# One written order for the loads, attention units and weight decodings of the opening, with the scaling of maxima and the reciprocals joined

## The chip, the cores and the metric

The kernel runs on one core of a Trainium2 chip. The metric is device time in microseconds (us) of one execution; of several runs the median is taken. The engines are named as the profile names them: PE (TensorE, matrix products; PEld its weight loads), DVE (VectorE), ACT (ScalarE), POOL (GpSimd) and SP (SyncE, whose queue issues every transfer of this kernel).

## What is computed

Three layers in a row, all in float32: windowed attention with 32 global tokens, a feed-forward layer with ELU, then a gated layer with an RMS norm.

```python
def reference(**kwargs):
    attn_out = _attn_ref(...)            # 4 batches, 8 heads, 512 local + 32 global tokens, head size 64
    x = attn_out.transpose(0, 2, 1, 3).reshape(B * S, H * D)      # 2176 tokens x 512
    x = _moe_ref(x, w_in, w_out)
    return _moe2_ref(x, w_gate, w_val, w_out, rms_g)

def _attn_ref(...):
    ...
    s_ll = np.where(np.abs(pos[:, None] - pos[None, :]) <= 32, s_ll, -1e9)
    s_l = np.concatenate([s_lg, s_ll], axis=-1)
    out_l = np.matmul(sm(s_l), np.concatenate([v_g, v_l], axis=2))
    # sm: e = exp(s - max); e / (sum(e) + 1e-9)

def _moe_ref(x, w_in, w_out):            # 512 -> 2048 -> 512
    h = x @ w_in
    return np.where(h > 0, h, np.exp(np.minimum(h, 0)) - 1) @ w_out

def _moe2_ref(x, w_gate, w_val, w_out, rms_g):
    xn = x / np.sqrt(mean(x * x) + 1e-6) * rms_g
    return (silu(xn @ w_gate) * (xn @ w_val)) @ w_out
```

The weights of the last two layers come as float64, 1 MB for 128 rows of two 512-column pieces.

## The kernel before

**Tiles and stages.** Local tokens are worked on in four blocks of 512 (one batch each). A block has four attention units of 128 tokens, so unit u belongs to block u // 4. The attention of the first block's units 0 to 3 runs ahead of everything else; units 4 to 7 run inside the feed-forward of block 0, and so on. After the fourth block comes the gated layer. The first 145 us or so hold the opening (units 0 to 3) and block 0, and the change lies in the first half of these.

**An attention unit** (lines 218 to 280): `a_S` makes two halves of scores (by `par`) in PSUM on PE; `a_E` takes the row maxima of each half on DVE (line 243), multiplies them by -1/8 (line 244), and lets ACT make the exponentials E (line 246); `a_T` turns E on PE (line 252) and ACT copies the result to ET (line 254); `a_PV` multiplies with the values (line 265); `a_N` adds 1e-9 to the sums (line 278), takes reciprocals (line 279) and scales the output into x (line 280), on DVE, one half after the other. `a_X` turns a whole block's x into xT on PE, with its high part on ACT (line 289) and its low part on DVE (line 290).

**A decoding** makes one 128x1024 piece of weights ready: ACT takes the absolute value of the float64's high word (line 83, "abs"), four DVE operations make the float32 of it (lines 90 to 93), ACT rounds to a high part (line 96, "hi") and DVE takes the low part (line 99, "lo"). Decodings are numbered in the order of `order1`: of each four, the first two are of `w_in` and serve four steps of a block, the other two are of `w_out` and serve two steps each. Two `dx` tiles hold the decodings under way, so the abs of decoding i + 2 waits for the lo of decoding i.

**A step j of a block** (16 in all, `moe_block`): `mm1` (line 132, 12 matmuls) makes h; `act1` makes g of it, with ReLU and exponential on ACT (lines 121, 122), a DVE operation (line 123), the high part on ACT (line 139) and the low part on DVE (line 140); `mm2` of the step before (line 146, 12 matmuls) adds to y. `att_slot` puts a unit among four steps: `a_S` and `a_E` in the first, behind `mm1`; `a_T` in the second, between the halves of `mm2`; `a_PV` and `a_N` in the third, behind `mm1`. The scores of unit 5 lie in step 4, those of unit 6 in step 8, those of unit 7 in step 12. Two PSUM buffers (tag `att`) serve `a_S`, `a_T` and `a_PV` of these units in turn, so the scores of unit 5 need the outputs of unit 4 read by `a_N`.

**What sets the order.** PE's order is written by the program. On DVE, ACT and SP a scheduler sets it, except in the opening, where DVE and ACT follow the program's lines (a `manual_schedule` from the casts of the constants to the lo of decoding 2). Each engine takes its instructions strictly in its own order: one that waits holds up all behind it. Step 0 to step 15 of block 0, with decodings 3 to 15, are the scheduler's. Line 75 issues a load of weights, line 205 one of a unit's keys and queries (`kq`), line 215 one of its values (`v`).

Of the kernel before, what the change touches and what calls it, by code (L numbers as in the profile page):

```python
# [42 lines left out]
def fused_kernel(ctx: ExitStack, tc: tile.TileContext, kq, vl, gkq, gv, w_in, w_out, w_gate, w_val, w_o2, rms_g, consts, out):  # L43
# [43 lines left out]

    def dec_bits(x, raw):
        word = words(raw)
        nc.vector.tensor_scalar(out=x, in0=x, scalar1=HI_MIN, scalar2=HI_MAX, op0=ALU.max, op1=ALU.min)  # L90
        nc.vector.tensor_scalar(out=i32(x), in0=i32(x), scalar1=3, scalar2=0x3FFFFFFF, op0=ALU.logical_shift_left, op1=ALU.bitwise_and)
        nc.vector.scalar_tensor_tensor(out=i32(x), in0=word[:, :, 1], scalar=-0x40000000, in1=i32(x), op0=ALU.bitwise_and, op1=ALU.bitwise_or)  # L92
        nc.vector.scalar_tensor_tensor(out=i32(x), in0=word[:, :, 0], scalar=29, in1=i32(x), op0=ALU.logical_shift_right, op1=ALU.bitwise_or)  # L93
# [989 lines left out]
```

## Time and profile before

| | us |
|---|---|
| median of 3 runs (899.44 to 900.13) | 899.59 |
| the profiled execution | 899.1 |
| its span in the profile | 897.3 |
| PE busy | 864.9 (96%) |
| DVE busy | 588.0 (66%) |
| ACT busy | 475.8 (53%) |

A span is the time from the first to the last instruction in the profile. Busy PE is not PE at its peak, since ends of matmuls are modelled; what counts here is where PE stands still, and in whose queue the instruction stands that it waits for. Of the 32 us in which PE is not busy, 22 lie in the first 70 us.

### The profile page before, as it was taken

What the parts mean: (1) busy time and instruction counts of PE and PEld (TensorE: products, weight loads), DVE (VectorE), ACT (ScalarE), POOL (GpSimd) and SP (SyncE); (2) the same over time, 40 slices, a digit from 0 to 9 for tenths busy, and PEclk for the clock granted to TensorE, in tenths of its full rate; (3) what the DMA queues carried; (4) which work ended last, traced back from release to release, by engine and by line L of the source; (5) the groups of instructions that cost most, each with busy time, mean ns of one, the idle gap of its engine ahead of it and who ended that gap; (6) DMA issues with size and microseconds to landing.
All of it is one profiled execution on the core that took longest, in us unless ns stands there. A gap on an engine that the chain in (4) does not pass through costs nothing.

```text
span 897.3 us, 16243 instructions
## 1 busy us (share of the span) xinstructions
PE 864.9 (96%) x6652; PEld 736.4 (82%) x6652; DVE 588.0 (66%) x983; ACT 475.8 (53%) x863; POOL 19.4 (2%) x22
## 2 busy tenths in 40 slices
PE   4789999999999999999999999999999999999997
PEld 3567877888888888677888899997999998899995
DVE  4899988777677764443488656885355776365642
ACT  4677664555564444333456655664455665355531
POOL 0000000000000000000110101000100000000000
PEclk8999999999999999999999999999999999999999
DMA  9786365966678742441405532233222232133200
GB/s 361 289 305 198 124 255 178 300 229 203 228 273 267 248 163 112 148 177 60 167 1 188 179 114 91 96 120 118 81 96 94 95 119 80 59 118 118 95 24 35
DMA packets 60225, 139.26 MB, mean 155 GB/s; under 512 B 4856, under 2 KB 30584, under 8 KB 57592
## 3 DMA queue, kind: packets, MB, share of 16 engines
q1 hardware_dynamic: 60152, 138.23, 44.7%
q8 instruction: 52, 0.85, 0.4%
q14 instruction: 21, 0.17, 0.1%
HBM read 115.15 MB, written 23.07 MB: 154 GB/s over the span
## 4 chain that ended last, share of the span: by engine, by line
PE 79%; DVE 11%; DMA 4%; ACT 3%; issue 1%; SPq 0%; POOL 0%; ACTq 0%
PE y L146 16%; PE A L739 15%; PE h L132 15%; PE o L745 15%; PE Q L739 11%; DMA kq<-in_kq 2%; DVE dx L93 2%; DVE dx L92 1%; PE s L234 1%; PE ptp L252 1%; DVE wA L99 1%; PE o L265 1%; PE hg L675 1%; DMA raw<-in_moe_w_out 1%; DVE dx L90 1%
## 5 line engine op out<-in xcount | busy, mean ns | idle before, releaser
L146 PE MATMUL y<-g,wA 128*128 128x512 f32 x768 | 197.3, 400 | 4.7 <-DVE g L140 4.1
L132 PE MATMUL h<-xT,wA 128*128 128x512 f32 x768 | 186.5, 391 | 1.7 <-DVE xT L290 1.7
L146 PEld LDWEIGHTS y<-g,wA 128*128 128x128 f32 x768 | 140.0, 189 | 40.2 <-DVE g L140 6.0
L132 PEld LDWEIGHTS h<-xT,wA 128*128 128x128 f32 x768 | 143.5, 188 | 32.7 <-DVE xT L290 2.4
L739 PE MATMUL A<-xc,wS 128*128 128x384 f32 (+1 forms) x864 | 155.9, 328 | 1.7 <-ACT t L931 0.9
L739 PEld LDWEIGHTS A<-xc,wS 128*128 128x128 f32 x864 | 145.0, 188 | 6.6 <-ACT t L931 1.3
L745 PE MATMUL o<-wB,p 128*128 128x512 f32 x612 | 147.3, 392 | 0.7 <-DVE p L750 0.3
L745 PEld LDWEIGHTS o<-wB,p 128*128 128x128 f32 x612 | 113.6, 188 | 24.7 <-DVE p L750 2.5
L739 PE MATMUL Q<-xc,wS 128*128 128x384 f32 (+1 forms) x648 | 115.3, 326 | 0.0
L739 PEld LDWEIGHTS Q<-xc,wS 128*128 128x128 f32 x648 | 107.8, 188 | 0.0
L595 DVE TENSOR_TENSOR wS<-wraw,wS 128x1024 fp32r<-128x1024 f32 x63 | 78.5, 1246 | 36.2 <-ACT wS L594 36.0
L754 DVE TENSOR_TENSOR t<-t,Q 128x384 f32<-128x384 f32 (+1 forms) x108 | 55.9, 528 | 37.2 <-PE Q L739 24.0
L594 ACT CAST wS<-wraw 128x1024 fp32r<-128x1024 f32 x63 | 65.9, 1050 | 19.6 <-PE Q L739 11.4
L121 ACT ACTIVATE e<-h 128x512 f32<-128x512 f32 x48 | 29.0, 605 | 69.8 <-PE h L132 69.7
L139 ACT CAST g<-e 128x512 fp32r<-128x512 f32 x64 | 39.8, 621 | 47.3 <-DVE e L123 30.8
L123 DVE SCALAR_TENSOR_TENSOR e<-e,h 128x512 f32<-128x512 f32 x48 | 32.5, 678 | 33.3 <-ACT e L122 33.3
L140 DVE TENSOR_TENSOR g<-e,g 128x512 fp32r<-128x512 f32 x64 | 43.8, 684 | 9.4 <-ACT g L139 9.1
L750 DVE TENSOR_TENSOR p<-p,p 128x384 fp32r<-128x384 f32 x36 | 20.0, 557 | 43.1 <-ACT p L749 43.1
L83 ACT ACTIVATE dx<-raw 128x1024 f32<-128x1024 f32 x34 | 39.2, 1157 | 15.9 <-DMA raw<-in_moe_w_gate 6.0
L90 DVE TENSOR_SCALAR dx<-dx 128x1024 f32<-128x1024 f32 x34 | 23.2, 688 | 33.7 <-ACT dx L83 33.7
L246 ACT ACTIVATE E<-s,mx 128x128 f32<-128x128 f32 x128 | 34.8, 385 | 17.2 <-DVE mx L244 17.2
L92 DVE SCALAR_TENSOR_TENSOR dx<-raw,dx 128x1024 int32<-128x1024 int32 x34 | 41.9, 1239 | 0.6
(173 smaller groups left out, 867.1 us busy)
## 6 DMA issues: line engine op xcount, KB each, us to landing
wraw<-wS SPq DMA_DIRECT2D x63, 512.0 KB, 3.2
raw<-in_moe_w_out SPq DMA_DIRECT2D x14, 1024.0 KB, 7.6
raw<-in_moe_w_in SPq DMA_DIRECT2D x8, 1024.0 KB, 6.0
raw<-in_moe_w_gate SPq DMA_DIRECT2D x6, 1024.0 KB, 6.6
raw<-in_moe_w_val SPq DMA_DIRECT2D x6, 1024.0 KB, 5.7
wS<-raw SPq DMA_DIRECT2D x48, 128.0 KB, 2.4
gvr<-in_gv SPq DMA_DIRECT2D x8, 640.0 KB, 4.7
wS<-dx SPq DMA_DIRECT2D x36, 128.0 KB, 2.1
```

The costliest lines, as they stand in the source:

```text
L83: ins = nc.scalar.activation(x, f(words(raw)[:, :, 1]), AF.Abs)
L92: nc.vector.scalar_tensor_tensor(out=i32(x), in0=word[:, :, 1], scalar=-0x40000000, in1=i32(x), op0=ALU.bitwise_and, op1=ALU.bitwise_or)
L132: nc.tensor.matmul(h[:, :n], W1[c, G][:, ws, o:o + P], xT[c][:, xs, :n], start=(k == 0), stop=(k == 11))
L139: nc.scalar.copy(g[:, 0, :n], e[:, :n])
L140: nc.vector.tensor_tensor(out=g[:, 1, :n], in0=e[:, :n], in1=f(g[:, 0, :n]), op=ALU.subtract)
L146: nc.tensor.matmul(ys[dc][:, :n], W2[j][:, ws, dc * P:(dc + 1) * P], g[:, gs, :n], start=(j == 0 and k == 0), stop=(j == 15 and k == 2))
L246: nc.scalar.activation(e[par][:, pr, :], ss[par][:, pr, :], AF.Exp, bias=mx[:, par, pr:pr + 1], scale=SCALE)
L594: nc.scalar.copy(t[:, :, 0, :], raw)
L595: nc.vector.tensor_tensor(out=t[:, :, 1, :], in0=raw, in1=f(t[:, :, 0, :]), op=ALU.subtract)
L739: nc.tensor.matmul(ps[:, :n], w[:, 2 * (q % 4) + c, ws, :], x[:, c, xs, :n], start=(first and c == 0 and z == 0), stop=(c == 1 and z == 2) ...
L745: nc.tensor.matmul(o, p[:, pp, t * P:(t + 1) * P], Wo[j][:, ww, :], start=(first and z == 0), stop=(last and z == 2))
L754: nc.vector.tensor_tensor(out=t, in0=t, in1=ps, op=ALU.add)
```

## The change

The opening and steps 0 to 3 of block 0 are written out in two lists: `LOADS` for SP's queue, and `STEPS` for PE, DVE and ACT together. The helpers are cut into single operations for it (`dec_bit` is one of the four DVE operations of a decoding; `e_max`, `e_scale`, `e_exp`; `n_add`, `n_rec`, `n_mul`; `x_tr`, `x_hi`, `x_lo`), and `moe_block(0, ...)` begins at step 4. In `STEPS` a name is an operation and a number: mx, sc, exp, T, ET, PV, ad, rc, N belong to a unit (a and b are its halves), abs, ba, bb, bc, bd, hi, lo to a decoding, relu, ex, stt, ghi, glo to a step. Seven decodings (0 to 6) stand in the list, 5 ahead of 4. What follows the list on DVE and ACT is still the scheduler's, which may also put later operations between those of the list.

In every unit, of the list or not, the two multiplications by -1/8 are one (both halves, 128x8), and so are the two reciprocals; both maxima then come ahead of any exponential, and both sums ahead of any scaling of outputs. The condition that decodings in block 0 are issued after the last part of xT (`issue_after`) is gone.

```diff
+        def e_max(u, par):
+            if u not in mx_t:
+                mx_t[u] = small.tile([P, 2, 4], F32, tag="st", name="mx")
+            nc.vector.tensor_reduce(out=mx_t[u][:, par, :], in_=s_t[u][par], axis=AX.X, op=ALU.max)
+
+        def e_scale(u):
+            nc.vector.tensor_scalar(out=mx_t[u], in0=mx_t[u], scalar1=-SCALE, scalar2=None, op0=ALU.mult)
...
         def a_E(u):
-            ss = s_t.pop(u)
-            mx = small.tile([P, 2, 4], F32, tag="st", name="mx")
-            e = [ap_.tile([P, 4, P], F32, tag=f"E{par}", name="E") for par in range(2)]
-            for par in range(2):
-                nc.vector.tensor_reduce(out=mx[:, par, :], in_=ss[par], axis=AX.X, op=ALU.max)
-                nc.vector.tensor_scalar(out=mx[:, par, :], in0=mx[:, par, :], scalar1=-SCALE, scalar2=None, op0=ALU.mult)
-                for pr in range(4):
-                    nc.scalar.activation(e[par][:, pr, :], ss[par][:, pr, :], AF.Exp, bias=mx[:, par, pr:pr + 1], scale=SCALE)
-            e_t[u] = e
+            e_max(u, 0)
+            e_max(u, 1)
+            e_scale(u)
+            e_exp(u, 0)
+            e_exp(u, 1)
...
+        def a_N(u):
+            n_add(u, 0)
+            n_add(u, 1)
+            n_rec(u)
+            n_mul(u, 0)
+            n_mul(u, 1)
...
-        def moe_block(b, slot, after=None):
+        def moe_block(b, slot, j0=0, ys=None, prev=None):
...
+        LOADS = """
+            mk kq0 ident kq1 raw0 kq2 v0 raw1 kq3 v2 v1 raw2 v3 raw3 v4 raw5 kq4 raw6 raw4
+        """.split()
+        STEPS = """
...
+            bd6 ghi3 glo3 hi6 rc4 N4b lo6 N4a
+        """.split()
...
+        with tc.manual_schedule(engines={mybir.EngineType.SP}):
+            for what in LOADS:
+                start_load(what)
         with tc.manual_schedule(engines={mybir.EngineType.DVE, mybir.EngineType.Activation}):
...
+            for what in STEPS:
+                start_step(what)
+                if what in ("lo2", "lo3", "lo5", "lo6"):
+                    w1_load()
...
             if part == 2:
-                with tc.issue_after(last[0].ins), tc.issue_after(last[1].ins):
-                    w1_decode()
+                w1_decode()
...
-        moe_block(0, slot0)
+        moe_block(0, slot0, 4, y0, gs_[3])
```

**The order at three places.** From the scores of unit 5 on, PE has the same instructions in the same order as before. First, the head of SP's queue: before, the loads of values alternate with those of keys and queries.

```order
L205 DMA kq0_102<-in_kq 128x1408
L349 DMA ident_83<-in_consts 128x128
L350 DMA mk_104<-in_consts 128x384
L75 DMA raw_108<-in_moe_w_in 128x2x512
L215 DMA v0_110<-in_vl 128x2080
L205 DMA kq0_116<-in_kq 128x1408
L215 DMA v0_118<-in_vl 128x2080
L75 DMA raw_120<-in_moe_w_in 128x2x512
```

And the head of SP's queue now:

```order
L453 DMA mk_103<-in_consts 128x384
L213 DMA kq0_111<-in_kq 128x1408
L455 DMA ident_83<-in_consts 128x128
L213 DMA kq0_114<-in_kq 128x1408
L75 DMA raw_116<-in_moe_w_in 128x2x512
L213 DMA kq0_118<-in_kq 128x1408
L223 DMA v0_120<-in_vl 128x2080
L75 DMA raw_122<-in_moe_w_in 128x2x512
```

The masks and the keys and queries of units 0 to 2 moved ahead of the first values.

Second, DVE around the end of unit 4, whose two scalings (`x` from `o` and `st`) set free the PSUM that the scores of unit 5 are written to. Before, they stand among decodings 4 (`dx_794`, `wA_800`) and 5 (`dx_881`, `wA_887`):

```order
L99 TENSOR_TENSOR wA_800<-dx_794,wA_800 128x2x512
L278 TENSOR_SCALAR st_860<-o_826 128x4
L93 SCALAR_TENSOR_TENSOR dx_881<-raw_645,dx_881 128x1024
L279 RECIPROCAL st_860<-st_860 128x4
L123 SCALAR_TENSOR_TENSOR e_818<-e_818,h_805 128x512
L279 RECIPROCAL st_860<-st_860 128x4
L90 TENSOR_SCALAR dx_924<-dx_924 128x1024
L280 TENSOR_TENSOR x_859<-o_825,st_860 128x4x64
L280 TENSOR_TENSOR x_859<-o_826,st_860 128x4x64
L99 TENSOR_TENSOR wA_887<-dx_881,wA_887 128x2x512
```

Now (`dx_903`, `wA_917` are decoding 6, `dx_1018` is decoding 7; `g_914` belongs to step 3, `e_941` to step 4):

```order
L97 SCALAR_TENSOR_TENSOR dx_903<-raw_142,dx_903 128x1024
L95 SCALAR_TENSOR_TENSOR dx_1018<-raw_664,dx_1018 128x1024
L525 TENSOR_TENSOR g_914<-e_906,g_914 128x512
L299 RECIPROCAL st_863<-st_863 128x8
L131 SCALAR_TENSOR_TENSOR e_941<-e_941,h_928 128x512
L97 SCALAR_TENSOR_TENSOR dx_1018<-raw_664,dx_1018 128x1024
L306 TENSOR_TENSOR x_920<-o_829,st_863 128x4x64
L107 TENSOR_TENSOR wA_917<-dx_903,wA_917 128x2x512
L306 TENSOR_TENSOR x_920<-o_812,st_863 128x4x64
```

The scalings of unit 4 moved behind all of decoding 6, the four bit operations of decoding 7, and the DVE operation of step 4.

Third, DVE around the maxima of unit 6, for which its exponentials, and then its transposes on PE in step 9, wait. Before:

```order
L99 TENSOR_TENSOR wA_1218<-dx_1212,wA_1218 128x2x512
L99 TENSOR_TENSOR wA_1320<-dx_1314,wA_1320 128x2x512
L123 SCALAR_TENSOR_TENSOR e_1236<-e_1236,h_1223 128x512
L243 TENSOR_REDUCE mx_1285<-s_1243 128x4
L243 TENSOR_REDUCE mx_1285<-s_1244 128x4
L90 TENSOR_SCALAR dx_1371<-dx_1371 128x1024
L90 TENSOR_SCALAR dx_1455<-dx_1455 128x1024
L244 TENSOR_SCALAR mx_1285<-mx_1285 128x4
```

Now:

```order
L131 SCALAR_TENSOR_TENSOR e_1227<-e_1227,h_1214 128x512
L97 SCALAR_TENSOR_TENSOR dx_1444<-raw_1169,dx_1444 128x1024
L251 TENSOR_REDUCE mx_1276<-s_1234 128x4
L251 TENSOR_REDUCE mx_1276<-s_1235 128x4
L91 TENSOR_SCALAR dx_1485<-dx_1485 128x1024
L148 TENSOR_TENSOR g_1231<-e_1227,g_1231 128x512
L107 TENSOR_TENSOR wA_1450<-dx_1444,wA_1450 128x2x512
L254 TENSOR_SCALAR mx_1276<-mx_1276 128x8
```

The scaling of unit 6's maxima stood behind decodings 0 to 11 and the first operation of 12 and 13; now it stands behind decodings 0 to 13 and the first operation of 14.

## Rows read from the trace of the kernel before

**Rows 1.** Order of time on PE: start us, busy us, [idle before and its releaser].

```profile
36.32 1.64 PE L288 MATMUL xtp<-ident,x 128*128 128x128 f32 x13 [0.73 <-DVE x L280]
...
50.33 1.80 PE L146 MATMUL y<-g,wA 128*128 128x512 f32 x5 [2.56 <-DVE g L140]
...
66.37 2.81 PE L146 MATMUL y<-g,wA 128*128 128x512 f32 x11 [0.96 <-DVE g L140]
...
71.83 0.40 PE L228 MATMUL s<-masks,identr 128*32 128x256 bf16 x8
...
106.63 1.04 PE L252 MATMUL ptp<-ident,E 128*128 128x128 f32 x8
```

**Rows 2.** Stretches: start:end us, length, busy of PE, PEld, DVE, ACT, POOL, PEclk, DMA share, GB/s.

```profile
48.00:50.00 2.00, 0.00 (x0) 0.00 (x0) 2.00 (x3) 1.84 (x4) 0.00 (x0) 1.00 0.97 373
...
52.00:54.00 2.00, 2.00 (x10) 1.68 (x10) 1.97 (x4) 1.91 (x6) 0.00 (x0) 0.50 1.02 418
```

**Rows 3.** DVE by line, 0 to 63.9 us: xcount | busy us, mean ns | idle before, releaser.

```profile
L92 DVE SCALAR_TENSOR_TENSOR dx<-raw,dx 128x1024 int32<-128x1024 int32 x6 | 7.4, 1242 | 0.1
L93 DVE SCALAR_TENSOR_TENSOR dx<-raw,dx 128x1024 int32<-128x1024 int32 x6 | 7.3, 1218 | 0.1
...
L99 DVE TENSOR_TENSOR wA<-dx,wA 128x1024 fp32r<-128x1024 f32 x5 | 6.1, 1212 | 2.3 <-ACT wA L96 2.3
L90 DVE TENSOR_SCALAR dx<-dx 128x1024 f32<-128x1024 f32 x7 | 4.7, 681 | 9.8 <-ACT dx L83 9.8
...
L91 DVE TENSOR_SCALAR dx<-dx 128x1024 int32<-128x1024 int32 x6 | 4.1, 690 | 0.1
L290 DVE TENSOR_TENSOR xT<-xtp,xT 128x512 fp32r<-128x512 f32 x4 | 2.5, 684 | 1.0 <-ACT xT L289 1.0
L123 DVE SCALAR_TENSOR_TENSOR e<-e,h 128x512 f32<-128x512 f32 x3 | 2.0, 660 | 0.0
L279 DVE RECIPROCAL st<-st 128x4 f32<-128x4 f32 x10 | 1.7, 175 | 0.3
L244 DVE TENSOR_SCALAR mx<-mx 128x4 f32<-128x4 f32 x10 | 1.7, 166 | 0.3
...
L140 DVE TENSOR_TENSOR g<-e,g 128x512 fp32r<-128x512 f32 x2 | 1.4, 682 | 0.0
```

**Rows 4.** DVE by line, 0 to 104.25 us, the same columns.

```profile
L92 DVE SCALAR_TENSOR_TENSOR dx<-raw,dx 128x1024 int32<-128x1024 int32 x12 | 14.6, 1227 | 0.1
L93 DVE SCALAR_TENSOR_TENSOR dx<-raw,dx 128x1024 int32<-128x1024 int32 x12 | 14.5, 1215 | 0.1
L99 DVE TENSOR_TENSOR wA<-dx,wA 128x1024 fp32r<-128x1024 f32 x12 | 14.5, 1212 | 2.4 <-ACT wA L96 2.3
L90 DVE TENSOR_SCALAR dx<-dx 128x1024 f32<-128x1024 f32 x14 | 9.4, 681 | 9.8 <-ACT dx L83 9.8
...
L91 DVE TENSOR_SCALAR dx<-dx 128x1024 int32<-128x1024 int32 x12 | 8.1, 684 | 0.1
...
L140 DVE TENSOR_TENSOR g<-e,g 128x512 fp32r<-128x512 f32 x8 | 5.4, 679 | 0.0
```

**Rows 5.** Order of time on DVE.

```profile
46.13 1.21 DVE L93 SCALAR_TENSOR_TENSOR dx<-raw,dx 128x1024 int32<-128x1024 int32 x1
47.27 1.27 DVE L243 TENSOR_REDUCE mx<-s 128x4 f32<-128x512 f32 x2
48.47 1.20 DVE L99 TENSOR_TENSOR wA<-dx,wA 128x1024 fp32r<-128x1024 f32 x1
...
63.24 0.74 DVE L280 TENSOR_TENSOR x<-o,st 128x256 f32<-128x256 f32 x2
...
104.19 0.16 DVE L244 TENSOR_SCALAR mx<-mx 128x4 f32<-128x4 f32 x1
```

**Rows 6.** Order of time on ACT.

```profile
104.44 2.18 ACT L246 ACTIVATE E<-s,mx 128x128 f32<-128x128 f32 x8 [0.39 <-DVE mx L244]
```

**Rows 7.** Stretches, as in rows 2.

```profile
20.00:22.00 2.00, 1.06 (x64) 0.84 (x64) 1.86 (x7) 2.00 (x7) 0.00 (x0) 0.88 1.00 419
```

More of the change, by code (lines that the diff above doesn't have):

```diff
@@ L86, in dec_abs, with dec_bit @@
         return x
[L88 to L93 removed]
+    def dec_bit(k, x, raw):
+        word = words(raw)
+        if k == "a":
+            nc.vector.tensor_scalar(out=x, in0=x, scalar1=HI_MIN, scalar2=HI_MAX, op0=ALU.max, op1=ALU.min)
+        elif k == "b":
+            nc.vector.tensor_scalar(out=i32(x), in0=i32(x), scalar1=3, scalar2=0x3FFFFFFF, op0=ALU.logical_shift_left, op1=ALU.bitwise_and)
+        elif k == "c":
+            nc.vector.scalar_tensor_tensor(out=i32(x), in0=word[:, :, 1], scalar=-0x40000000, in1=i32(x), op0=ALU.bitwise_and, op1=ALU.bitwise_or)
+        else:
+            nc.vector.scalar_tensor_tensor(out=i32(x), in0=word[:, :, 0], scalar=29, in1=i32(x), op0=ALU.logical_shift_right, op1=ALU.bitwise_or)
+    def dec_bits(x, raw):
+        for k in "abcd":
+            dec_bit(k, x, raw)
     def split_hi(dst, t):
@@ L269, in a_N, with pv @@
-        def a_N(u):
-            b, T = u // 4, u % 4
-            if T == 0:
+        def pv(u, par, pool, tag):
+            ets, v = et_t.pop((u, par)), v_t[u]
+            o = pool.tile([P, 4, 65], F32, tag=tag, name="o")
+            for pr in range(4):
+                for i in range(4):
+                    nc.tensor.matmul(o[32 * i:32 * i + 32, pr, :], ets[:, pr * P + 32 * i:pr * P + 32 * i + 32], v[:, i, 2 * pr + par, :],
+                                     start=True, stop=True)
+            o_t[u, par] = o
@@ new lines, in a_PV, with n_add, n_rec, n_mul @@
+        def a_PV(u, pools):
+            for par in range(2):
+                pv(u, par, *pools[par])
+        def n_add(u, par):
+            if u not in st_t:
+                st_t[u] = small.tile([P, 2, 4, 2], F32, tag="st", name="st")
+            nc.vector.tensor_scalar(out=st_t[u][:, par, :, 0:1], in0=o_t[u, par][:, :, 64:65], scalar1=1e-9, scalar2=None, op0=ALU.add)
+        def n_rec(u):
+            nc.vector.reciprocal(st_t[u][:, :, :, 1:2], st_t[u][:, :, :, 0:1])
+        def n_mul(u, par):
+            b, T = u // 4, u % 4
+            if b not in x_t:
@@ L290, in a_X, with x_tr @@
-                lo = nc.vector.tensor_tensor(out=xT[c][:, 1, :], in0=pt, in1=f(xT[c][:, 0, :]), op=ALU.subtract)
-            return hi, lo
+                pt = x_tr(b, c, *pools[c])
+                x_hi(xT, c, pt)
+                x_lo(xT, c, pt)
+        def x_tr(b, c, pool, tag):
+            pt = pool.tile([P, 512], F32, tag=tag, name="xtp")
+            for T in range(4):
+                nc.tensor.transpose(pt[:, T * P:(T + 1) * P], x_t[b][:, T, c * P:(c + 1) * P], ident)
+            return pt
@@ L302, in att_slot @@
             if jj == 1 and part == 1:
-                a_T(u, 0, aps, "att")
-                a_T(u, 1, aps, "att")
+                for par in range(2):
+                    a_ET(u, par, a_T(u, par, aps, "att"))
             if jj == 2 and part == 0:
@@ new lines, in fused_kernel, with start_load @@
+        """.split()
+        HB = [(hps, "h")] * 2
+        mk = moe.tile([P, 3, P], F32, tag="e", name="mk", bufs=2)
+        xT_t = {0: new_xT()}
+        pts, gs_, hs_, es_, y0 = {}, {}, {}, {}, []
+        def start_load(what):
+            if what == "mk":
+                nc.sync.dma_start(out=mk, in_=consts[:, 0:3 * P].rearrange("p (a b) -> p a b", a=3))
+            elif what == "ident":
+                nc.sync.dma_start(out=ident, in_=consts[:, 3 * P:4 * P])
+            else:
+                i = int(what.lstrip("kqvraw"))
+                if what[0] == "r":
+                    wp = i % 2 == 1
+                    raws[i] = dec_load(wpool if wp else dec["r"], "w" if wp else "raw", w_src(*order1[i]))
+                else:
+                    (load_kq if what[0] == "k" else load_v)(i)
```

172 lines of the change are left out of this document (89 added, 83 removed).

## The prediction, made before the changed kernel was run

> **What bounds the kernel now.** I read four views: PE in order of time, to see where it stands still; stretches with DVE's load and the granted clock; DVE by line, to count what its queue has done by a given moment; and DVE and ACT in order of time around the waits. PE waits for DVE: 2.56 us for the low part of a step's g ending at 50.33, 0.96 us ending at 66.37 [rows 1]. DVE is busy 2.00 of 2.00 us in one of these stretches and 1.97 in another [rows 2]. From 66.37 on PE hardly pauses, so a microsecond by which PE is earlier or later at the end of the opening and of block 0 is a microsecond of the kernel. The question is therefore not how much DVE work the change saves, but when the operations that PE waits for come out of DVE's queue, since an engine takes its queue in order.
>
> **What the change saves on DVE.** I call s the time by which DVE reaches the same amount of work earlier.
> - Start: DVE stands 9.8 us in all for an absolute value, nearly all ahead of its first decoding [rows 3]. Now the maxima of units 0 and 1 come ahead of it, for which only the masks, `ident` and two `kq` loads are needed. DVE can start some 1.2 us earlier (an estimate: three loads, 0.98 MB, at 419 GB/s [rows 7] are no sooner in than before; bounds 0 and 3).
> - Joined operations: five scalings and five reciprocals less by the end of unit 4, 0.166 and 0.175 us busy [rows 3], 5 x 0.166 + 5 x 0.175 = 1.7 us. The lower bound is 0.7: between two other operations such a short one takes less than its busy time, as a 1.21 us operation takes 1.14 from start to start (46.13 to 47.27 [rows 5]). I take 1.7, since in units 0 to 3 each of them waited for the one ahead.
> - Waits in the opening: 2.3 us for high parts and 1.0 for those of xT [rows 3]. The interleaved list removes these, but puts in waits for loads: at 419 GB/s [rows 7] the values of unit 3, after 10.55 MB, land at some 25 us plus the first 3 to 5, while the DVE list would be at unit 3's sums by 30 to 31. I take a gain of 1.4 (bounds -2 and 3.3).
> - Operations that depend on the one ahead are parted by others: some 0.6 us (bounds 0 and 1).
> - New waits on ACT cost DVE some 0.7 us (bounds 0 and 2): the absolute value of decoding 7 stands behind the ReLU of step 3, and needs the low part of decoding 4 first.
>
> So s = 1.2 + 1.7 + 1.4 + 0.6 - 0.7 = 4.2 us. The bounds together would be -3.3 and 9; not all fall to one side, so I use 1.5 to 8.
>
> [...]
>
> **What the new order costs.** I price from start to start: 1.14 us for the 1024-wide operations of lines 92, 93 and 99, 0.60 for lines 90, 91, 123 and 140 (two maxima of that class take 47.27 to 48.47 [rows 5]).
>
> First place: the scores of unit 5. Before, the scalings of unit 4 run 63.24 to 63.98 [rows 5], and PE comes to the scores only at 71.83 [rows 1], without a wait. By then DVE had done 7, 6, 6 and 6 of the bit operations, 5 low parts of weights, 3 and 2 operations of steps [rows 3]. Now 8 of each bit operation, 7 low parts and 5 and 4 operations of steps stand ahead of them. That is 3 bit operations at 0.60 and 4 at 1.14, 2 low parts at 1.14, 4 step operations at 0.60: 1.8 + 4.56 + 2.28 + 2.4 = 11.0 us more. The scalings end at 63.98 + 11.0 - 4.2 = 70.8. PE will have finished `mm1` of step 4 by about 65 (xT begins some 3 us earlier than at 36.32 [rows 1], since the opening's sums are done by 33), so it stands still for some 5 us, and starts the scores of unit 5 only 1.0 us earlier than before. Queued behind on PE are `mm2` of step 3 and everything else.
>
> Second place, and the one that decides: unit 6. Before, the first scaling of its maxima ends at 104.35 [rows 5], ACT's exponentials run 104.44 to 106.62 [rows 6], and PE's transposes start at 106.63 [rows 1], with no wait shown. DVE had done 14, 12, 12 and 12 bit operations, 12 low parts and 8 low parts of g [rows 4]. Now 15, 14, 14 and 14, 14, and 9 stand ahead of the one scaling: 4 x 0.60 + 6 x 1.14 = 9.24 us more. It ends at 104.35 + 9.24 - 4.2 = 109.4, the exponentials at 109.4 + 2.2 = 111.6. The second four of the eight transposes began at about 106.63 + 0.5 = 107.1 before; now they begin at 111.6. PE is 4.5 us late there. Behind them stand the second half of `mm2` of step 8 and the rest of the kernel.
>
> Between the two places the same thing happens in smaller measure (the scaling of unit 5 stands behind decoding 8 and three operations of 9), so PE loses its 1.0 us and comes late by steps. After unit 6, decodings 0 to 13 are done and little is left in DVE's queue, so nothing more is lost; and nothing is won back, since PE's work from there on is the same and without pauses of any size. What is won on DVE ends as idle time of DVE.
>
> [...]
>
> **Sum.** 899.1 (span 897.3 and what lies around it) + 4.5 = 903.6 against the profiled execution. The median of the runs shown, 899.59, is 0.5 above that execution, so I forecast 903.8, between the two ways of placing it.
>
> **Rivals.**
> [...]
> - *No measurable difference.* s is 7 to 8, because the opening's waits nearly all go: then unit 6 is 0.7 to 1.7 us late, 900.6. For it: 9.8 and 3.3 us of DVE's idle time [rows 3] are there to be taken. Against: the loads still bring the same bytes at the same rate.
> - *Faster.* The opening was bound by its loads and its start, not by DVE's work, and the new orders let DVE begin near 7 us and never wait: 3 + 1.7 + 3.3 + 1 and some of the work behind the later loads, s = 12. Then unit 6 is on time and PE keeps the difference beyond 9.24 + 0.5: 899.1 - 2.2 = 896.9. It decides from s = 9.8 on. Against: the bounds above add up to 9.
> - *The list does not hold*, because the scheduler moves its operations: the orders in which the engines' instructions stand show that it holds, with later operations put between. I give this no chance of its own.
>
> **How the numbers follow.** Forecast 58% (901.4 to 905.9), deeper 15% (906 to 908), no difference 20% (897.8 to 901.4), faster 7%. About 0.2%, 1.8 us, is what a measurement of this kernel can tell from no change. Faster by more than that 0.07, within it 0.20, slower 0.73. The range leaves out the fast case, half of the lowest third and the far end of the deep one: 900.0 to 907.0.
>
> **What the changed profile would show.** Right: a pause of PE of 3 to 6 us ahead of the scores of unit 5, ended by DVE's scaling into x; waits of PE for exponentials at the transposes of units 5 and 6; the transposes of unit 6 at 110 to 112 us; DVE full from 35 to 110 us and then with more idle time than before; xT begun near 33. Wrong: unit 4's scalings ending before 66, or the transposes of unit 6 starting before 107; then s is larger than I think, and the time is at or below 899.6. If the transposes are late but the kernel is not, PE has later pauses that absorb it, which the trace of before does not show me.

## The result, and the profile after

The changed kernel is slower: 907.07 us median of 6 runs (906.16 to 912.16) against 899.52 us for the kernel before in 6 runs beside it (899.19 to 900.13), a ratio of 1.0091, 95% interval 1.0069 to 1.0114. The profiled execution took 907.48 us, its span 905.6 us, 8.3 more than before.

PE of the changed kernel in order of time, the answer to [rows 1] (start us, busy us, idle before and its releaser). L306 is the scaling of a unit's output into x on DVE, L259 an exponential on ACT, L332 the low part of xT on DVE:

```profile
36.80 1.64 PE L325 MATMUL xtp<-ident,x 128*128 128x128 f32 x13 [0.55 <-DVE x L306]
40.45 3.01 PE L140 MATMUL h<-xT,wA 128*128 128x512 f32 x12 [2.02 <-DVE xT L332]
...
72.57 0.41 PE L236 MATMUL s<-masks,identr 128*32 128x256 bf16 x4 [4.36 <-DVE x L306]
74.03 0.41 PE L236 MATMUL s<-masks,identr 128*32 128x256 bf16 x4 [1.06 <-DVE x L306]
74.37 1.96 PE L242 MATMUL s<-kq__711 64*32 64x128 f32 x64
76.25 4.93 PE L154 MATMUL y<-g,wA 128*128 128x512 f32 x12
...
86.26 0.66 PE L272 MATMUL ptp<-ident,E 128*128 128x128 f32 x4 [0.98 <-ACT E L259]
87.30 0.66 PE L272 MATMUL ptp<-ident,E 128*128 128x128 f32 x4 [0.38 <-ACT E L259]
...
114.46 0.66 PE L272 MATMUL ptp<-ident,E 128*128 128x128 f32 x4 [0.28 <-ACT E L259]
115.50 0.66 PE L272 MATMUL ptp<-ident,E 128*128 128x128 f32 x4 [0.38 <-ACT E L259]
```

The pause ahead of the scores of unit 5 is there (4.36 and 1.06 us), then a wait for exponentials at the transposes of unit 5, and again at those of unit 6. The second four transposes of unit 6 begin at 115.50 instead of some 107.1: 8.4 us late, as much as the spans differ (8.3).

DVE of the changed kernel, in order of time, as in [rows 5]:

```profile
9.55 1.29 DVE L251 TENSOR_REDUCE mx<-s 128x4 f32<-128x512 f32 x2 [8.68 <-PE s L242]
...
72.10 0.41 DVE L306 TENSOR_TENSOR x<-o,st 128x256 f32<-128x256 f32 x1
72.44 1.21 DVE L107 TENSOR_TENSOR wA<-dx,wA 128x1024 fp32r<-128x1024 f32 x1
73.57 0.41 DVE L306 TENSOR_TENSOR x<-o,st 128x256 f32<-128x256 f32 x1
...
83.91 0.17 DVE L254 TENSOR_SCALAR mx<-mx 128x8 f32<-128x8 f32 x1
...
113.02 0.15 DVE L254 TENSOR_SCALAR mx<-mx 128x8 f32<-128x8 f32 x1
113.09 0.68 DVE L93 TENSOR_SCALAR dx<-dx 128x1024 int32<-128x1024 int32 x1
```

And ACT, as in [rows 6], at the exponentials of unit 5, which stand behind an absolute value, and at those of unit 6, which wait for the scaling at 113.02:

```profile
84.02 1.16 ACT L83 ACTIVATE dx<-raw 128x1024 f32<-128x1024 f32 x1 [2.41 <-DVE wA L107]
85.07 2.17 ACT L259 ACTIVATE E<-s,mx 128x128 f32<-128x128 f32 x8
...
113.26 2.18 ACT L259 ACTIVATE E<-s,mx 128x128 f32<-128x128 f32 x8 [2.54 <-DVE mx L254]
```

The scalings of unit 4 end at 73.98 instead of 63.98, the scaling of unit 6's maxima at 113.17 instead of 104.35. DVE by line up to 113.1 us, the answer to [rows 4] (count, busy us, mean ns, idle before and its releaser):

```profile
L95 DVE SCALAR_TENSOR_TENSOR dx<-raw,dx 128x1024 int32<-128x1024 int32 x14 | 17.1, 1222 | 0.1
L107 DVE TENSOR_TENSOR wA<-dx,wA 128x1024 fp32r<-128x1024 f32 x14 | 17.0, 1219 | 0.6 <-ACT wA L104 0.6
L97 DVE SCALAR_TENSOR_TENSOR dx<-raw,dx 128x1024 int32<-128x1024 int32 x14 | 17.0, 1216 | 0.1
...
L91 DVE TENSOR_SCALAR dx<-dx 128x1024 f32<-128x1024 f32 x15 | 10.3, 687 | 0.5 <-ACT dx L83 0.4
L251 DVE TENSOR_REDUCE mx<-s 128x4 f32<-128x512 f32 x14 | 9.1, 683 | 10.0 <-PE s L242 10.0
...
L296 DVE TENSOR_SCALAR st<-o 128x4 f32<-128x4 f32 x12 | 1.8, 158 | 3.7 <-PE o L285 3.7
```

The counts are those that the order promised (14, 14 and 14 of the operations at 1.14 us, 15 of each at 0.60). What the forecast did not have is in the last column: DVE waits 3.7 us for outputs of PE in the opening. The stretches behind the pause, as in [rows 2]:

```profile
72.00:74.00 2.00, 0.41 (x4) 0.13 (x5) 2.00 (x5) 1.37 (x2) 0.00 (x0) 0.50 1.03 422
74.00:76.00 2.00, 1.97 (x68) 1.61 (x67) 2.00 (x3) 1.09 (x2) 0.00 (x0) 0.50 0.85 346
...
78.00:80.00 2.00, 2.00 (x6) 1.52 (x6) 2.00 (x3) 0.00 (x0) 0.00 (x0) 0.50 0.76 304
```

PE's granted clock is 0.50 from 72 to 80 us, while DVE is busy throughout (1.97 to 2.00 us of each 2.00).

How late PE is against the kernel before, by the start of the first matmul of each group (us from the start of each span, worked out from the traces; minus is earlier):

| kernel | scores 5 | transposes 5 | scores 6 | transposes 6 | scores 7 | block 1, first scores |
|---|---|---|---|---|---|---|
| changed | +0.74 | +6.06 | +7.40 | +7.83 | +8.80 | +7.72 |
| join_only | +0.57 | +1.50 | +1.28 | +3.49 | +5.64 | +4.54 |
| unit4_early | -3.70 | -1.95 | -1.52 | +0.08 | +2.65 | +1.58 |
| decode_later | -3.76 | -2.40 | -1.32 | -1.33 | -1.52 | -1.70 |
| join_held | +2.86 | +2.83 | +2.80 | +2.81 | +3.54 | +5.10 |
| both_later_slack | -4.27 | -4.28 | -3.01 | -2.99 | -2.28 | -1.92 |

### The profile page after: what moved, and what is told of

Same layout as the page of the kernel before. It is cut to its first block, busy times and chain, and to the rows that moved or that the text cites. A ratio compares the mean times of both kernels' runs of the same rounds, so it can differ in the third digit from the quotient of the medians.

```text
span 905.6 us, 16198 instructions
## 1 busy us (share of the span) xinstructions
PE 868.9 (96%) x6652; PEld 738.5 (82%) x6652; DVE 586.9 (65%) x951; ACT 476.3 (53%) x863; POOL 19.4 (2%) x22
## 4 chain that ended last, share of the span: by engine, by line
PE 79%; DVE 11%; DMA 4%; ACT 3%; issue 2%; POOL 0%; SPq 0%; ACTq 0%; DVEq 0%
PE y L154 16%; PE A L824 15%; PE h L140 15%; PE o L830 14%; PE Q L824 11%; DMA v<-in_vl 2%; DVE dx L95 2%; PE o L285 1%; DVE dx L97 1%; DVE wA L107 1%; PE s L242 1%; PE ptp L272 1%; PE hg L760 1%; DVE dx L93 1%; DVE dx L91 1%
## 5 line engine op out<-in xcount | busy, mean ns | idle before, releaser
L129 ACT ACTIVATE e<-h 128x512 f32<-128x512 f32 x44 | 26.7, 607 | 73.1 <-PE h L140 73.0
L147 ACT CAST g<-e 128x512 fp32r<-128x512 f32 x60 | 37.5, 624 | 44.7 <-DVE e L131 28.4
L131 DVE SCALAR_TENSOR_TENSOR e<-e,h 128x512 f32<-128x512 f32 x44 | 30.0, 681 | 42.6 <-ACT e L130 42.6
L83 ACT ACTIVATE dx<-raw 128x1024 f32<-128x1024 f32 x34 | 39.5, 1162 | 18.2 <-DVE wA L107 7.2
L148 DVE TENSOR_TENSOR g<-e,g 128x512 fp32r<-128x512 f32 x60 | 40.9, 682 | 10.4 <-ACT g L147 10.0
L259 ACT ACTIVATE E<-s,mx 128x128 f32<-128x128 f32 x128 | 35.2, 390 | 13.9 <-DVE mx L254 12.3
L95 DVE SCALAR_TENSOR_TENSOR dx<-raw,dx 128x1024 int32<-128x1024 int32 x34 | 42.1, 1238 | 0.6
L97 DVE SCALAR_TENSOR_TENSOR dx<-raw,dx 128x1024 int32<-128x1024 int32 x34 | 41.4, 1219 | 0.4
```

Of the source, the lines that this page charges most:

```text
L83: ins = nc.scalar.activation(x, f(words(raw)[:, :, 1]), AF.Abs)
L147: nc.scalar.copy(g[:, 0, :n], e[:, :n])
L148: nc.vector.tensor_tensor(out=g[:, 1, :n], in0=e[:, :n], in1=f(g[:, 0, :n]), op=ALU.subtract)
```

## The experiments

The theory under test: what counts is how much DVE work stands ahead of the few operations that PE waits for. Rivals: the new order of the loads, the joined operations themselves, and PE's pause with the lower clock behind it (granted 0.50 from 72 to 80 us in the changed kernel). All ratios are to the kernel before on the same chip; its median there was 899.8 to 900.5 us.

| run | median us | ratio | 95% interval |
|---|---|---|---|
| join_only | 905.08 | 1.0066 | 1.0041 to 1.0092 |
| values_first | 912.48 | 1.0141 | 1.0119 to 1.0162 |
| unit4_early | 902.08 | 1.0024 | 1.0007 to 1.0041 |
| decode_later | 900.33 | 1.0004 | 0.9991 to 1.0017 |
| join_held | 905.13 | 1.0052 | 1.0034 to 1.0071 |
| six_ops_less | 901.83 | 1.0025 | 1.0014 to 1.0036 |
| both_moves | 900.27 | 1.0000 | 0.9990 to 1.0009 |
| both_moves_xT | 901.51 | 1.0009 | 0.9993 to 1.0025 |
| later_and_slack | 898.18 | 0.9982 | 0.9970 to 0.9994 |
| both_later_slack | 897.90 | 0.9980 | 0.9971 to 0.9990 |
| best_unjoined | 897.50 | 0.9970 | 0.9958 to 0.9983 |
| more_matmuls | 908.51 | one run | |

For the argument I counted the DVE work that stands ahead of two operations in the order of each kernel's DVE instructions, priced as the prediction did (from start to start, 1.14 and 0.60 us and 0.37 for a scaling into x; 0.17, its busy time, for a short operation), and set it against the measured end:

| kernel | end of unit 4: work, measured, rest | unit 6's scaling: work, measured, rest |
|---|---|---|
| before | 47.4, 63.98, 16.6 | 88.4, 104.35, 16.0 |
| changed | 56.7, 73.98, 17.3 | 95.6, 113.17, 17.6 |
| join_only | 49.2, 67.55, 18.4 | 89.8, 108.02, 18.2 |
| unit4_early | 44.5, 61.69, 17.2 | 86.9, 104.65, 17.8 |
| decode_later | 52.6, 69.52, 16.9 | 81.1, 101.07, 20.0 |
| six_ops_less | 49.3, 70.11, 20.8 | 84.7, 106.55, 21.9 |

The rest is DVE's start and its waits. Where DVE does not get ahead of PE it is nearly the same (16.0 to 18.4); in the other three it grows (20.0 to 21.9), because DVE then waits. From before to changed the work grows by 9.3 and 7.2 us, not by the prediction's 11.0 and 9.24, since here the joined operations are counted as saved.

### join_only: the joined operations alone, on the kernel before

```diff
-                nc.vector.tensor_scalar(out=mx[:, par, :], in0=mx[:, par, :], scalar1=-SCALE, ...)
+            nc.vector.tensor_scalar(out=mx, in0=mx, scalar1=-SCALE, scalar2=None, op0=ALU.mult)
...
-                nc.vector.reciprocal(st[:, par, :, 1:2], st[:, par, :, 0:1])
+            nc.vector.reciprocal(st[:, :, :, 1:2], st[:, :, :, 0:1])
```

> The kernel before, with the joined scaling of maxima and the joined reciprocals in every unit, and nothing else of the change (its opening keeps its order; from step 0 on the scheduler orders DVE anew). Queue theory (what counts is the DVE work that stands ahead of the scalings that PE waits for): counted with 0.60 and 1.14 us per operation, 89.8 us of DVE work stand up to the scaling of unit 6's maxima, where 88.4 stood up to the first of the two before and 95.6 in the changed kernel; so 0 to 1.5 us slower, 899.5 to 901. If joining itself were the loss: 905 to 908. If joining brings what the forecast counted, with nothing moved: 898 to 899.

Measured: 905.08 us. The expected 899.5 to 901 was wrong, and the time lies in the range of the rival that joining itself is the loss; by the ratios it is some seven tenths of the changed kernel's loss. What DVE waits for on PE's outputs in the first 37 us (us in total, times, longest), first in the kernel before, then in join_only:

```profile
DVE st L278 <- PE o L265: 0.6, 1, 0.6
```

```profile
DVE st L279 <- PE o L266: 2.8, 3, 2.0
```

Both sums now stand ahead of any scaling, so DVE waits for the second half of PE's products with nothing of the first half left to do: 2.2 us more. The ten operations saved are 1.7 us, and the last scaling of unit 3 ends at 36.93 instead of 36.26. From step 0 on the scheduler also puts more ahead of unit 6: 89.8 us of work instead of 88.4. Together 1.4 + 2.2 = 3.6 us, and unit 6's scaling is 3.67 us later; PE stands 1.83 us for the exponentials behind it at 110.12 (and 1.36 us for a low part of g at 124.23, behind unit 6, which the count does not have):

```profile
110.12 0.66 PE L253 MATMUL ptp<-ident,E 128*128 128x128 f32 x4 [1.83 <-ACT E L247]
```

### values_first: another order of the loads

```diff
-            mk kq0 ident kq1 raw0 kq2 v0 raw1 kq3 v2 v1 raw2 v3 raw3 v4 raw5 kq4 raw6 raw4
+            kq0 ident mk raw0 v0 kq1 v1 raw1 kq2 v2 kq3 v3 raw2 raw3 v4 raw5 kq4 raw6 raw4
```

> The changed kernel, with one list altered: the loads come as kq0, ident, mk, raw0, v0, kq1, v1, raw1, kq2, v2, kq3, v3, raw2, raw3 and then as they were, so that the values of units 0 and 1 land earlier; every engine's queue but that of the loads stays. Queue theory: the loads can only give back what the opening waits for them, at most the 2.1 and 2.0 us that PE waits for values at 26.08 and 31.84 us; unit 6's scaling then comes at 111 to 113 instead of 113.17, and the time is 905 to 907. Rival (the load order is what made the opening, and so the kernel, late): the whole 7.5 us come back, 899.5 to 901.

Measured: 912.48 us, slower than either theory said. PE no longer waits for values, but it waits longer for the keys and queries of the third unit (4.11 us instead of 2.08):

```profile
21.47 1.96 PE L242 MATMUL s<-kq 64*32 64x128 f32 x64 [4.11 <-DMA kq<-in_kq]
...
45.04 3.01 PE L140 MATMUL h<-xT,wA 128*128 128x512 f32 x12 [2.02 <-DVE xT L332]
```

The first step begins 4.6 us later than in the changed kernel (45.04 against 40.45), and the span is 4.5 us longer: the lateness of the opening goes to the end undiminished here. It shows what loads can cost, not that those of the changed kernel cost nothing; but the next runs keep them, and some of them end level with the kernel before or below it.

### unit4_early and decode_later: one piece of the order each

```diff
-            bb4 mm2_1 relu2 ad4a bc4 ex2 stt2 bd4 ghi2 mm1_3 glo2 hi4 lo5 mm2_2 ad4b abs6 lo4 ...
-            bd6 ghi3 glo3 hi6 rc4 N4b lo6 N4a
+            bb4 mm2_1 relu2 ad4a bc4 ex2 stt2 bd4 ghi2 mm1_3 glo2 hi4 ad4b rc4 N4b N4a lo5 mm2_2 abs6 lo4 ...
+            bd6 ghi3 glo3 hi6 lo6
```

> The changed kernel with the four operations that finish unit 4 (second sum, reciprocals, two scalings) taken from the end of the list to a place ahead of the low part of decoding 5; loads and joined operations stay. Queue theory: DVE work up to the end of unit 4 falls from 56.7 to 44.5 us, up to the scaling of unit 6's maxima from 95.6 to 86.9; with 17.5 us of start and waits, as in the changed kernel, these come at 62 and 104.5, no pause ahead of the scores of unit 5, transposes of unit 6 at 106 to 107: 899 to 901. Rivals: loads or joining carry the loss, 905 to 907.

```diff
             if part == 2:
-                w1_decode()
+                with tc.issue_after(sc_i[4 + j // 4].ins):
+                    w1_decode()
```

> The changed kernel, with each decoding of steps 4 to 15 issued behind the scaling of the maxima of the unit of those four steps; the list, the loads and the joined operations stay. Queue theory: DVE work up to the end of unit 4 is 52.6 us (56.7 in the changed kernel), so its scalings end at 70 and PE still pauses some 2 us ahead of the scores of unit 5; up to the scaling of unit 6's maxima it is 81.1 instead of 95.6, so the transposes of unit 6 don't wait: 899 to 901.5. Rival (the pause ahead of unit 5 and the clock after it carry the loss): 904 to 907. Rival (loads or joining): 905 to 907.

Measured: 902.08 us, some 1 us above the range expected, and 900.33 us, within it. Either move brings back most of the loss with the same loads and the same joined operations. unit4_early ends unit 4 at 61.69 and scales unit 6's maxima at 104.65, both within 0.5 us of what was counted; it keeps a wait of 0.67 us at the transposes of unit 6 and two around 120 us (1.23 and 0.32), so it stays 2 us short. decode_later has the pause ahead of unit 5 (0.40 and 1.21 us), no wait at unit 6, and PE is 1.7 us ahead of the kernel before at the end of block 0. It loses this at 167 us (1.04 us in the row shown and 0.33 us behind it). PE first, then ACT:

```profile
167.05 0.50 PE L154 MATMUL y<-g,wA 128*128 128x512 f32 x1 [1.04 <-ACT g L147]
```

```profile
165.27 1.23 ACT L83 ACTIVATE dx<-raw 128x1024 f32<-128x1024 f32 x1 [3.73 <-DMA raw<-in_moe_w_val]
166.38 0.61 ACT L147 CAST g<-e 128x512 fp32r<-128x512 f32 x1
```

The absolute value of a weight whose load is not there stands 3.73 us at the head of ACT's queue, and the high part of a step's g stands behind it.

### join_held: joined operations, decodings held back, on the kernel before

```diff
-                with tc.issue_after(last[0].ins), tc.issue_after(last[1].ins):
+                with tc.issue_after(last[0].ins), tc.issue_after(last[1].ins), tc.issue_after(sc_i[4 + j // 4].ins if 4 <= j < 12 else last[0].ins):
                     w1_decode()
```

> The kernel before with the joined operations (as join_only), and with each decoding of steps 4 to 11 issued behind the scaling of that unit's maxima. It parts the two prices of joining: the operations' own, and that of the new order in which the scheduler puts decodings around them. Queue theory: up to the scaling of unit 6's maxima 81.1 us of DVE work stand instead of 89.8; with 18.3 us of start and waits, as in join_only, that is 99.4, so the transposes don't wait, and only the opening's 0.7 us (join_only's first step begins 0.67 us later) and a wait of the same size remain: 900 to 901.5. Rival (joining itself holds PE up, since both maxima have to be there before the first exponential): 904 to 906, as join_only.

Measured: 905.13 us; the expected 900 to 901.5 was wrong, and the time lies in the range of the rival. At unit 6 the theory holds for PE, which is 2.8 us late at the scores of unit 5 and still 2.8 at the transposes of unit 6, without a wait there. The scaling of unit 6's maxima comes at 105.99 and not at the 99.4 counted: DVE waits 4.7 us for outputs of PE and 3.9 us for ACT's exponentials of steps up to there. And the work held back meets PE at the next place:

```profile
136.33 1.42 PE L146 MATMUL y<-g,wA 128*128 128x512 f32 x5 [1.34 <-DVE g L140]
```

Holding moves the wait to unit 7 unless some DVE work goes behind unit 7 as well; decode_later does that with the last decoding. The 2.8 us at unit 5 are 0.8 of a later start (PE's first matmul at 7.87 instead of 7.06 us, with the same loads ahead), 1.1 in the opening and 0.9 around unit 4; for the last no cause is shown. So neither this run nor join_only clears the joined operations: both are some 5 us slower than the kernel before, and what of this is joining by itself stays open.

### six_ops_less: less DVE work in the same list

```diff
-                dec_bit(kind[1], dxs[i], raws[i])
+                if not (kind in ("bc", "bd") and i in (4, 5, 6)):
+                    dec_bit(kind[1], dxs[i], raws[i])
```

> The changed kernel without the last two of the four bit operations of decodings 4, 5 and 6: six DVE operations of 1.14 us, 6.8 us, are left out (these weights are then not decoded in full); the orders stay, but for what the scheduler fills in behind. Queue theory: DVE work up to the end of unit 4 falls from 56.7 to 49.3 us, up to the scaling of unit 6's maxima from 95.6 to 84.7; with 17.5 us of start and waits, unit 4 ends at 66.8, the scaling comes at 102 to 103, PE waits at neither place: 899.5 to 901.5. Rival (loads or the opening carry the loss; DVE's work is not what counts): 905 to 907.

Measured: 901.83 us, just above the range expected: 6.8 us of DVE work left out give back some 5 us. Unit 4 ends at 70.11 rather than 66.8 and the scaling of unit 6's maxima comes at 106.55 rather than 102 to 103, so PE still waits a little at both places (0.30 and 1.17 us, 0.77 and 0.38 us). DVE starts 1.0 us later in this execution and waits 3.2 us between 37 and 70 us, where the changed kernel shows no wait. So DVE's work was the bound, until its own inputs were.

### both_moves, both_moves_xT: the two moves together

both_moves has the diffs of unit4_early and decode_later, but the last decoding is not held (`if j < 12`). both_moves_xT has in addition

```diff
-            ... N3a N3b abs3 bb2 X01 bc2 X23 xh1 xh0 xl1 xh2 xl0 xh3 xl2 xl3 bd2 mm1_0 ba3 hi2 bb3 lo2 bc3 abs5 S4 bd3
-            relu0 ex0 mm1_1 mx4a hi3 stt0 mx4b ghi0 sc4 glo0
+            ... N3a N3b bb2 X01 xh0 xh1 X23 xl0 xh2 xl1 xh3 xl2 xl3 abs3 bc2 bd2 mm1_0 ba3 hi2 bb3 lo2 bc3 S4 bd3
+            relu0 ex0 mm1_1 stt0 ghi0 mx4a glo0 hi3 mx4b sc4 abs5
```

> The changed kernel with both moves: unit 4's last operations early in the list, as in unit4_early, and decodings of steps 4 to 11 behind the scaling of that unit's maxima, as in decode_later, but the last decoding left free. Queue theory: 44.5 us of DVE work up to the end of unit 4, 81.1 up to the scaling of unit 6's maxima; no wait of PE at either place, and the 1.5 to 2 us by which PE was ahead at unit 7 in decode_later are not given back in the second block: 897 to 899.5. Rival (what decode_later gave back at 167 us comes from the loads of the third layer's weights, whatever the last decoding does): 899.5 to 901.

> both_moves, and in the list the parts of xT come right behind their transposes (the absolute value of decoding 3 and one bit operation of decoding 2 go behind them), and the work on the g of step 0 ahead of the maxima of unit 4. In the changed kernel PE waits 2.02 us for xT at 40.45 and 1.08 + 0.25 us for this g at 48.89; about 0.7 and 1.3 us of these can go. Queue theory: DVE has slack for PE in both_moves, so PE keeps 1 to 2 us of it: 895.5 to 898.5. Rival (a later wait takes it back): as both_moves.

Measured: 900.27 and 901.51 us, no gain over the kernel before, and both above what was expected. PE of both_moves is 3.8 us ahead at unit 5, and loses it at weights and at unit 7, where the last decoding stands ahead again:

```profile
94.65 1.19 PE L140 MATMUL h<-xT,wA 128*128 128x512 f32 x4 [1.06 <-DVE wA L107]
...
131.05 1.43 PE L154 MATMUL y<-g,wA 128*128 128x512 f32 x5 [1.39 <-DVE g L148]
```

In both_moves_xT the first step does begin 0.9 us earlier (39.47 against 40.36), but the first `mm2` only 0.2 us: it waits 1.67 us for ACT's high part of g instead of 1.08, and its next 11 matmuls then take 4.22 us (from 49.29), 2.83 in both_moves (from 49.54).

### later_and_slack, both_later_slack, best_unjoined: versions that beat both kernels

later_and_slack is decode_later with

```diff
+        tasks.insert(4, ("n",))
...
                 what, *of = tasks.pop(0)
+                if what == "n":
+                    return
```

> decode_later, and the tasks that prepare the third layer's weights have one empty place ahead of the second decoding of w_val, so that everything behind it comes one step later. In decode_later PE was 1.7 us ahead of the kernel before at 159.8 us and lost it at 167 to 168 us: ACT stood 3.73 us for the load of that piece, with the high part of a step's g queued behind it. Queue theory: with the absolute value one step later on ACT, PE keeps the 1.7 us, and the time is 1 to 2 us below before: ratio 0.998 to 0.999. Rival (the gain is lost at another wait, as at the first products of the third layer, where PE waits 0.94 us in before and 1.93 us in decode_later): ratio 1.000.

both_later_slack adds the diff of unit4_early; best_unjoined is both_later_slack with

```diff
-            sc_i[u] = nc.vector.tensor_scalar(out=mx_t[u], in0=mx_t[u], scalar1=-SCALE, ...)
+            for par in range(2):
+                sc_i[u] = nc.vector.tensor_scalar(out=mx_t[u][:, par, :], in0=mx_t[u][:, par, :], scalar1=-SCALE, ...)
...
-            nc.vector.reciprocal(st_t[u][:, :, :, 1:2], st_t[u][:, :, :, 0:1])
+            for par in range(2):
+                nc.vector.reciprocal(st_t[u][:, par, :, 1:2], st_t[u][:, par, :, 0:1])
```

> later_and_slack, with unit 4's last operations early in the list, as in unit4_early. In decode_later PE paused 0.40 and 1.21 us ahead of the scores of unit 5; these go. Queue theory: the two moves add only as far as DVE has slack up to unit 7: the same DVE work stands ahead of the scaling of unit 7's maxima (107.0 us in both), so no more than 0.5 us is won over later_and_slack: ratio 0.997 to 0.999. Rival (pauses of PE add up): 1.6 us more than later_and_slack, ratio 0.996.

> both_later_slack, with the scalings of maxima and the reciprocals in two pieces each again, one per half, in all units (both still behind the later maximum or sum). DVE then has 10 short operations more up to the end of unit 4 and 16 more up to the scaling of unit 7's maxima. If joining saves DVE what the forecast counted, 0.17 us each, in a queue that is on time for PE: 46.2 instead of 44.5 us of work up to unit 4, 109.6 instead of 107.0 up to unit 7, and as PE has little slack there 1 to 2.6 us slower, ratio 0.999 to 1.001. If a short operation costs its 0.07 us between two others: 0.5 to 1 us slower, ratio 0.998 to 0.999. If joining brings nothing here: ratio 0.998.

Measured: 0.9982, 0.9980 and 0.9970, all faster than the kernel before by the intervals. The wait at 167 us is gone, and what PE has ahead at unit 7 it keeps. The second move adds nothing that can be told, as the same DVE work stands ahead of unit 7. Nor does taking the joined operations apart again cost anything: having fewer operations brings nothing here. The parted ones still stand behind the later maximum or sum, so this run does not test the wait for the later half. Who PE waits for between 37 and 200 us in both_later_slack (us in total, times, longest):

```profile
PE h L140 <- DVE xT L332: 2.0, 1, 2.0
PE xtp L325 <- DVE xT L332: 1.4, 1, 1.4
PE h L140 <- DVE wA L107: 1.1, 1, 1.1
PE y L154 <- ACT g L523: 1.1, 1, 1.1
```

In the changed kernel the first of that table is 5.4 us for the scalings into x (L306), and 2.0 us for exponentials; both are gone here.

### more_matmuls: what PE stops for in the opening

```diff
-                for i in range(4):
+                for i in list(range(4)) * (5 if u == 0 else 1):
                     first, _, last = WBLK[i]
```

> The changed kernel with 32 more matmuls in the scores of unit 0 (the 8 that write the masks are issued five times; the result is the same). In five of the six profiles so far PE stops within its first 480 matmuls at the same counts, 348 to 350 and 474 to 476, whatever stands there, with nothing shown that it waits for, and goes on 1.2 to 1.4 us behind the start of a 16 KB packet of the instruction queue or of what follows it. If PE waits there for its own instructions, the second stop moves 32 matmuls back in the program, from the middle of unit 2's second products with the values (31.84 us in the changed kernel) to the start of the first ones. If it waits for data or for ACT, it stays at the second ones. The time of one look is 905 to 909 either way.

Measured: one run, 908.51 us. Counting PE's matmuls from the start, the stops ahead of the rows at 28.83 and 34.94 come behind 476 and 603 of them:

```profile
28.83 1.17 PE L285 MATMUL o<-v,ET 128*32 128x65 f32 x64 [0.31 <-issue]
...
34.94 0.31 PE L285 MATMUL o<-v,ET 128*32 128x65 f32 x5 [2.57 <-issue]
```

Unit 2's second products with the values, ahead of which the changed kernel stands 2.03 us, run without a stop. There is one behind 476 matmuls again, now at the start of unit 2's products, as expected of PE's own instructions, though it is short (0.31 us); a longer one follows behind 603, in the products of unit 3, where the changed kernel has none. The last section says what this means.

## Why the prediction was wrong, point by point

**Direction and mechanism: right.** Slower was given 73%. The pause ahead of the scores of unit 5 ended by the scaling into x (forecast 3 to 6 us, measured 4.36 + 1.06), waits for exponentials at units 5 and 6, DVE full from 35 to 110 us (busy 73.6 of 75) and nothing won back behind: all as written. The counts of what stands ahead (11.0 and 9.24 us) fit the orders, and six_ops_less, unit4_early and decode_later show that less work ahead of these operations brings PE back.

**Size: wrong, and the step is the term s**, the time by which DVE reaches the same work earlier. It was put at 4.2 us with 1.5 as the lower of the bounds used. Measured, it is 63.98 + 11.0 - 73.98 = 1.0 at the first place and 104.35 + 9.24 - 113.17 = 0.4 at the second. The unit 6 transposes at 115.50 rather than 111.6 are this error of 3.8 us; 899.1 + 4.5 + 3.8 = 907.4 would have been right. The lateness also came earlier than forecast: most of it is there at the transposes of unit 5 (+6.06), and unit 6, "the one that decides", added about 1 us (+7.40 at its scores, +7.83 and +8.4 at the two halves of its transposes).

**Its parts.** Start: DVE's first work is at 9.55 us, 10.21 in the kernel before: 0.7 instead of 1.2. Waits: behind the first operation DVE waited 4.6 us before (0.4 of the 9.8, 2.3 and 1.0 [rows 3], and 0.6 and 0.3 for PE); now it is 1.3 + 3.7 + 0.6 + 0.4 = 6.0 us up to unit 6's scaling. A gain of 1.4 was forecast, less 0.7 for new waits on ACT; a loss of 1.4 came: most waits for ACT went (3.7 us before, 1.0 now) and waits for PE took their place (0.9 before, 5.0 now). Joined and parted operations together are what is then left of the 0.4 at unit 6, 0.4 - 0.7 + 1.4 = 1.1 us, where 2.3 was forecast; and join_only shows the other side of joining: 2.2 us of waiting for the later half.

The forecast gave the opening to DVE and the loads. I read that PE had waits there but not for what. Of PE's waits in the first 45 us, two rows of the kernel before and three of the changed one:

```profile
PE s L234 <- DMA kq<-in_kq: 4.1, 2, 3.1
PE o L265 <- issue: 3.1, 2, 1.8
```

```profile
PE o L285 <- DMA v<-in_vl: 2.1, 1, 2.1
PE s L242 <- DMA kq<-in_kq: 2.1, 1, 2.1
PE o L285 <- ACT ET L277: 2.0, 1, 2.0
```

The new order of the loads did not shorten the waits for them: 4.1 us for keys and queries before, 2.1 for these and 2.1 for values now. A stop in which PE waits for nothing that the profile shows is still there: the 2.0 us, ahead of 31.84, are put down to a copy of ACT that began at 30.61, but by the list these products need the copy before that one, which began at 28.16. And PE itself was slower. Up to the last transpose for xT (37.96 us before, 38.44 now) it stood still for 14.9 us instead of 16.7, but was busy for 23.5 us instead of 21.3 (worked out from the two traces). At the end of the opening, from 34 to 36 us, its granted clock was 0.50, and 1.00 before; before, then now:

```profile
34.00:36.00 2.00, 1.59 (x67) 1.25 (x67) 1.85 (x7) 1.55 (x2) 0.00 (x0) 1.00 1.04 381
```

```profile
34.00:36.00 2.00, 2.00 (x59) 1.75 (x51) 0.91 (x5) 1.16 (x2) 0.00 (x0) 0.50 1.02 421
```

So xT began at 36.80 (its last 13 transposes), not 3 us earlier than at 36.32, and DVE, which needs PE's products, did not get ahead. The forecast had no term for PE's own pace in the opening; what the loads, the stop and the pace cost each by itself is not shown.

**The clock behind the pause.** PE's granted clock was 0.50 from 72 to 80 us, after PE had stood still from 68.2 us on, and the twelve matmuls at 76.25 took 4.93 us where the twelve of a step's `mm2` take 2.9 to 3.4 in the steps around it. The forecast's sum has no term for this. PE still waited 0.98 us for unit 5's exponentials, and DVE, full all the while (1.97 to 2.00 us of each 2.00 from 72 to 80 us), would not have reached their scaling earlier, so no cost of the slower matmuls is shown.

**Short operations.** A scaling between two others takes 0.07 us from start to start (113.02 to 113.09), and best_unjoined shows no loss from having more of them (ratio 0.9970, where both_later_slack has 0.9980).

**The rival of no difference** rested on opening waits that nearly all go; they did not. The deeper lateness (906 to 908 in the chances) had the right size. The absolute value of decoding 10 stands ahead of unit 5's exponentials on ACT, some 1.0 us, but it waits for a low part of weights (2.41 us) and not for a load. At unit 6 it is DVE's scaling alone that ACT waits for (2.54 us). Parting the loss between the joined operations and the list is not possible from these runs: joining made the scheduler write a new order, join_only and join_held came out where their rivals had them, and no run parts the operations in the changed kernel as it was. What is shown is that the order of DVE's work is enough to undo the loss: with the loads and the joined operations kept, decode_later takes back all of it that can be told (ratio 1.0004).

## What to carry to other kernels

Where one engine is full for a whole stage, count what stands in its queue ahead of the operations that another engine waits for, and move work behind all of these places, not only behind the next one. Give no credit for fewer operations, or for waits that go, until you know what the partner engine is late for; joining two operations of two halves makes both wait for the later half (2.2 us more of waiting in join_only). A queue's head that waits for a load costs what stands behind it (3.73 us on ACT at 165 us in decode_later, and 1.04 us of PE's time), so work that is ahead of its data belongs further back.
